# Loads mixed by size, a longer output lag, and one elementwise result kept in PSUM, in a fused attention and feed-forward kernel

## The chip, the cores and the metric

The kernel runs on one core of a Trainium2 chip. The metric is the device time of a run in microseconds (us). Kernels that are compared run on the same chip in the same rounds. A profile also gives the span of one execution; the time is 1.8 to 1.9 us longer than the span.

## The reference, cut to what matters

```python
# q, k, v: (8 batches, 8 heads, 576 positions, 64), float32
mask = np.abs(pos[:, None] - pos[None, :]) <= 32          # a window of 32 to each side
attn = softmax(where(mask, q @ k.T / 8, -1e9)) @ v
x = attn.transpose(0, 2, 1, 3).reshape(4608, 512)
h = x @ w_in                                              # 512 -> 2048
g = where(h >= 1, h, where(h <= -1, 0, (h + 1) ** 2 / 4)) # SMELU
out = g @ w_out                                           # 2048 -> 512, float32
```

The kernel writes SMELU as `min(r, 1) * max(h, r)` with `r = relu(0.5 h + 0.5)`: one ScalarE and two VectorE instructions.

## The kernel before

The main loop has 144 steps (18 blocks of 256 tokens, 8 column blocks of `w_in`). A step makes `hp` (eight matmuls), its SMELU into `gT`, and, LAG steps later, four matmuls into `op`. Attention work for later tokens (`sums`, `scores`) is laid into chosen steps. The mask is added on TensorE up to step 20 (`eng` is None); after that GpSimd multiplies the exponentials by a mask (`eng` is P).

```python
def load_long(b, half, t, eng=None, x=None):      # q or k of one token half: four loads of 72 KB
    ...
    for y in range(NY):
        (eng or nc.gpsimd).dma_start(out=x[32 * y:32 * y + 32], in_=...)
def load_w_in(n, c0=0, c1=512):                   # two loads, each over 64 partitions
    f = slice(512 * n + c0, 512 * n + c1)
    for h in range(2):
        nc.gpsimd.dma_start(out=w_in[64 * h:64 * h + 64, :, f], in_=...)
...
load_v(0, (1,))
load_w_in(0, 0, 256)
load_w_in(0, 256, 512)
load_w_in(1)
load_long(0, 1, 0)
load_long(0, 1, 1)
load_w_in(2)
load_w_in(3)
...
for a in range(NF * NB + LAG):                    # LAG = 12
    t, f = divmod(a, NF)
    eng = None if a < 21 else P
    ...
    if t < NB:
        ...
        hp = ps_h.tile([128, 2, TB], FP, name="hp", tag="hp")       # two buffers in PSUM
        ...                                                         # eight matmuls
        rr = ewp.tile([128, 2, TB], FP, name="rr")
        A.activation(rr, hp, AF.Relu, scale=0.5, bias=0.5)
        mx = ewp.tile([128, 2, TB], FP, name="mx")
        V.tensor_max(mx, hp, rr)
        V.scalar_tensor_tensor(gT[t][:, 2 * f:2 * f + 2], rr, 1.0, mx, op0=ALU.min, op1=ALU.mult)
    ...                                                             # sums and scores of the step
    if a >= LAG:
        for x in range(4 * (a - LAG), 4 * (a - LAG) + 4):
            tt, ff = divmod(x, 2 * NF)
            ...
            nc.tensor.matmul(op, gT[...], w_out[:, ff], start=ff == 0, stop=ff == 2 * NF - 1)
            if ff == 2 * NF - 1:                                    # every fourth step
                osb = osp.tile([128, DM], FP, name="osb")
                A.copy(osb, op)                                     # ScalarE
                nc.sync.dma_start(out=out[128 * tt:128 * tt + 128, :], in_=osb)
```

The softmax here doesn't subtract the row's maximum and nothing guards it: scores larger than these inputs give would overflow.

## Time and profile before

The median is 326.04 us. In the table, "start of step n" is the start of its first `hp` matmul in TensorE's timeline.

| Stage of the kernel before | us from the span's start |
|---|---|
| start of step 0, step 4, step 12 | 19.41, 27.90, 45.36 |
| steps 12 and 13 | 4.67 together |
| steps 14 to 29 | 36.30 |
| step 30 to the start of step 143 | 222.45 |
| start of step 143 to the end | 16.25 |

The prediction shows the page's slices, the waits and the timeline. Two lines of the page's costliest groups matter in addition. In such a line come source line, engine, operation, names and shapes, the count, after the bar the busy us and the mean ns of one, and after the second bar the idle time before them.

```profile
L424 DVE SCALAR_TENSOR_TENSOR gT<-rr,mx 128x512 bf16<-128x512 f32 x144 | 112.9, 784 | 4.9
L423 DVE TENSOR_TENSOR mx<-hp,rr 128x512 f32<-128x512 f32 x144 | 99.1, 688 | 35.5 <-ACT rr L421 34.6
```

The product is slower on average than the max (784 against 688 ns), because some products stand still beside a GpSimd mask.

### The profile page before, as it was taken

How to read it: one execution, taken by the hardware profiler on the slowest of the kernel's cores; microseconds unless marked ns; L12 is line 12 of the kernel's file. 1: busy time of each engine (PE TensorE's matmuls, PEld its weight loads, DVE VectorE, ACT ScalarE, POOL GpSimd, SP SyncE). 2: the span in 40 equal slices, each digit the busy share in tenths (PEclk: the TensorE clock that was granted, in tenths of full speed). 3: DMA queues.
4: the chain of work that ended last, by engine and by line, in shares of the span. 5: the costliest groups of instructions: out<-in, count | busy, mean ns of one | idle time of the engine just before them, and what ended most of it. 6: DMA issues, size and time to landing. Idle time of an engine off the chain costs nothing.

```text
span 325.0 us, 8421 instructions
## 1 busy us (share of the span) xinstructions
PE 301.7 (93%) x3575; PEld 203.2 (63%) x3619; DVE 238.8 (73%) x348; ACT 194.0 (60%) x318; POOL 142.1 (44%) x139
## 2 busy tenths in 40 slices
PE   8596799999999999999999999998999999999995
PEld 3354566666666666666666666666666666666652
DVE  2154787776878798978887787878787877887730
ACT  3455785676765766567655666665676666644421
POOL 8864914666454772457422952178232222100000
PEclk9987999999999999999999999999999999999999
DMA  9999997999969997699750999249960001110011
GB/s 145 117 146 168 127 206 132 147 133 167 84 124 140 88 148 146 89 85 158 127 107 34 120 159 163 58 55 169 138 136 34 34 34 41 52 41 32 34 65 65
DMA packets 129029, 34.52 MB, mean 106 GB/s; under 512 B 117728, under 2 KB 124128, under 8 KB 128992
## 3 DMA queue, kind: packets, MB, share of 16 engines
q0 software_dynamic: 100128, 18.06, 74.5%
q1 hardware_dynamic: 28864, 15.93, 20.4%
q8 instruction: 28, 0.46, 0.6%
q14 instruction: 9, 0.07, 0.1%
HBM read 36.70 MB, written 9.44 MB: 142 GB/s over the span
## 4 chain that ended last, share of the span: by engine, by line
PE 73%; POOL 7%; issue 6%; DVE 5%; DMA 4%; ACT 3%; POOLq 0%; ACTq 0%
PE hp L417 32%; PE op L439 31%; PE bb L280 5%; DMA w_in<-in_moe_w_in_dram 4%; DVE gT L424 2%; POOL vn L105 2%; PE bb L220 2%; DVE mx L423 2%; ACT pt L228 1%; POOL w_in L111 1%; POOL pt L230 1%; POOL kn L87 1%; PE tp L185 1%; POOL qn L95 1%; POOL kn L95 1%
## 5 line engine op out<-in xcount | busy, mean ns | idle before, releaser
L417 PE MATMUL hp<-xT,w_in 128*128 128x256 bf16 x1152 | 150.0, 274 | 5.1 <-DMA w_in<-in_moe_w_in_dram 2.8
L439 PE MATMUL op<-w_out,gT 128*128 128x512 bf16 x534 | 137.5, 379 | 5.8 <-issue 5.4
L417 PEld LDWEIGHTS <-w_in 128*128 128x128 bf16 x1152 | 112.0, 98 | 46.8 <-issue 5.9
L421 ACT ACTIVATE rr<-hp 128x512 f32<-128x512 f32 x144 | 85.8, 596 | 92.1 <-PE hp L417 87.8
L423 DVE TENSOR_TENSOR mx<-hp,rr 128x512 f32<-128x512 f32 x144 | 99.1, 688 | 35.5 <-ACT rr L421 34.6
L424 DVE SCALAR_TENSOR_TENSOR gT<-rr,mx 128x512 bf16<-128x512 f32 x144 | 112.9, 784 | 4.9
L230 POOL TENSOR_TENSOR pt<-pt,mask 128x1024 bf16<-128x1024 bf16 x24 | 53.2, 2218 | 83.9 <-ACT pt L228 79.0
L439 PEld LDWEIGHTS <-gT 128*128 128x128 bf16 x576 | 53.2, 98 | 42.1
L292 DVE TENSOR_TENSOR xT<-bb,rc 128x512 bf16<-128x512 f32 (+1 forms) x32 | 20.9, 653 | 22.7 <-ACT rc L287 22.7
L228 ACT ACTIVATE pt<-bb 128x1024 bf16<-128x1024 f32 (+1 forms) x33 | 33.1, 1011 | 6.8 <-PE bb L220 5.3
L443 ACT COPY osb<-op 128x512 f32<-128x512 f32 x36 | 21.0, 584 | 14.9 <-PE op L439 14.5
L105 POOL DMA_DIRECT2D vn<-in_v_dram x32 | 27.5, 897 | 0.0
L286 ACT ACTIVATE lr<-bb 128x512 f32<-128x512 f32 (+2 forms) x40 | 22.0, 549 | 3.8 <-PE bb L280 3.7
L287 ACT ACTIVATE rc<-lr 128x512 f32<-128x512 f32 (+2 forms) x40 | 23.5, 587 | 1.3
L280 PE MATMUL bb<-pt,ones 64*64 64x256 bf16 (+3 forms) x352 | 20.2, 260 | 2.7 <-POOL pt L230 1.2
L280 PE MATMUL bb<-pt,vn 64*64 64x128 bf16 (+3 forms) x712 | 19.0, 207 | 3.1 <-DMA vn<-in_v_dram 3.1
L248 POOL TENSOR_TENSOR pt<-pt,mask 128x384 bf16<-128x384 bf16 x7 | 6.4, 912 | 30.9 <-ACT pt L246 25.1
L280 PEld LDWEIGHTS <-vn 64*64 64x64 bf16 x712 | 17.3, 110 | 3.3 <-DMA vn<-in_v_dram 3.3
L280 PEld LDWEIGHTS <-ones 64*64 64x64 bf16 x352 | 10.8, 107 | 11.7 <-issue 8.3
L87 POOL DMA_DIRECT2D kn<-in_k_dram x16 | 8.7, 547 | 18.7 <-DMA w_in<-in_moe_w_in_dram 6.7
L95 POOL DMA_DIRECT2D qn<-in_q_dram x12 | 15.0, 1255 | 0.0
L95 POOL DMA_DIRECT2D kn<-in_k_dram x12 | 14.8, 1245 | 0.0
(46 smaller groups left out, 107.2 us busy)
## 6 DMA issues: line engine op xcount, KB each, us to landing
out_dram<-osb SPq DMA_DIRECT2D x36, 256.0 KB, 2.3
vn<-in_v_dram POOLq DMA_DIRECT2D x32, 144.0 KB, 8.1
qn<-in_q_dram POOLq DMA_DIRECT2D x12, 288.0 KB, 6.3
kn<-in_k_dram POOLq DMA_DIRECT2D x12, 288.0 KB, 8.4
w_out<-in_moe_w_out_dram POOLq DMA_DIRECT2D x4, 512.0 KB, 11.0
w_in<-in_moe_w_in_dram POOLq DMA_DIRECT2D x6, 256.0 KB, 7.6
kn<-in_k_dram POOLq DMA_DIRECT2D x16, 72.0 KB, 4.1
qn<-in_q_dram POOLq DMA_DIRECT2D x12, 72.0 KB, 8.0
```

The costliest lines, as they stand in the source:

```text
L95: nc.gpsimd.dma_start(out=x[:, :, h], in_=src[b, NY * h:NY * h + NY].rearrange("y s d -> (y s) d") .rearrange("(u p) d -> p u d", p=128))
L105: nc.gpsimd.dma_start(out=x[64 * a:64 * a + 64, :, h], in_=v[b, y:y + 2].rearrange("y s d -> (y s) d") .rearrange("(c r) d -> r c d", r=64))
L228: A.activation(p, ps[:, :, :128 * n].rearrange(like, y=m), AF.Exp, scale=D ** -0.5)
L230: eng.tensor_mul(p, p, mask4[:, :256 * n].rearrange("p (h j) -> p h j", h=2).rearrange(like, y=m))
L280: nc.tensor.matmul(bb[HD[h], a, o + c0:o + c1], ones[HD[a]] if c is None else vn[b][HD[a], c, h], p(a, h), start=n == 0, stop=True, skip_g ...
L286: A.activation(lr[:, :, :D0], bb[:, :, D0:2 * D0], AF.Ln)
L287: A.activation(rc[:, :, :D0], lr[:, :, :D0], AF.Exp, scale=-1.0)
L417: nc.tensor.matmul(hp[:, j], w_in[:, kk, 256 * f + 128 * j:256 * f + 128 * j + 128], xT[:, kk, r0:r0 + TB], start=n == 0, stop=n == 3)
L421: A.activation(rr, hp, AF.Relu, scale=0.5, bias=0.5)
L423: V.tensor_max(mx, hp, rr)
L424: V.scalar_tensor_tensor(gT[t][:, 2 * f:2 * f + 2], rr, 1.0, mx, op0=ALU.min, op1=ALU.mult)
L439: nc.tensor.matmul(op, gT[tt // 2][:, ff, 128 * (tt % 2):128 * (tt % 2) + 128], w_out[:, ff], start=ff == 0, stop=ff == 2 * NF - 1)
```

## The change

The intent has five parts. (1) All four first `v` loads come earlier, and small loads (72 KB) alternate with large ones in one queue order. (2) The output lag grows from 12 to 14. (3) Batch 2 is also loaded by token halves and transposed on TensorE. (4) The mask stays on TensorE up to step 27. (5) In the step after a GpSimd mask the max overwrites `hp` in PSUM, so that the product has only one input in SBUF.

```diff
-    load_v(0, (1,))
-    load_w_in(0, 0, 256)
-    load_w_in(0, 256, 512)
-    load_w_in(1)
-    load_long(0, 1, 0)
-    load_long(0, 1, 1)
-    load_w_in(2)
-    load_w_in(3)
...
+    for c in range(0, 512, 256):
+        for h in range(2):
+            load_w_in(c, c + 256, h)
+    def mix(small, large):
+        for n in range(0, max(len(small), 2 * len(large)), 2):
+            for fn, *x in large[n // 2:n // 2 + 1] + small[n:n + 2]:
+                fn(*x)
...
+    mix(halves(0, 1), [(load_w_in, c, c + 512, h) for c in (512, 1024, 1536) for h in range(2)])
+    mix(halves(1, 0), [(load_v, 1, n) for n in range(4)])
+    load_w_out(0)
+    load_w_out(1)
+    mix(halves(1, 1), [(load_w_out, 2), (load_w_out, 3)])
+    mix(halves(2, 0), [(load_v, 2, n) for n in range(4)])
...
-    LAG = 12
+    LAG = 14
+    PEM = 28
...
-    for n, a in enumerate((20, 22, 26, 28)):
+    for n, a in enumerate((20, 22, 25, 27)):
         at(a, seq[2 + n][0])
...
-    for n in range(3):
-        tps[23 + n] = [(2, n, t) for t in range(2)]
+    for b, half, *a in ((0, 1, 1, 3), (1, 0, 8, 9), (1, 1, 17, 18), (2, 0, 23, 24), (2, 1, 28, 29)):
+        for t in range(2):
+            tps[a[t]] = [(b, 2 * half + part, t) for part in range(2)]
...
+    masked = [a for a in ev if a >= PEM and any(x[0] is not sums for x in ev[a])]
...
-        eng = None if a < 21 else P
+        eng = None if a < PEM else P
...
-            mx = ewp.tile([128, 2, TB], FP, name="mx")
+            mx = hp if a - 1 in masked else ewp.tile([128, 2, TB], FP, name="mx")
```

More of the change, by code (lines that the diff above doesn't have):

```diff
@@ L45 @@
     PAD = 32
-    LONG, NAT = 2, 3
+    LONG = 3
     const = ctx.enter_context(tc.tile_pool(name="const", bufs=1))
@@ L78, with load_long @@
     qn, kn, vn = {}, {}, {}
-    def load_long(b, half, t, eng=None, x=None):
+    def load_long(b, half, t, y, eng=None, x=None):
         src, dst, nm = ((q, qn, "qn"), (k, kn, "kn"))[t]
-        if x is None:
-            x = nat.tile([128, 2, S], BF, name=nm, tag=nm + "l", bufs=3)
-        dst[b, half] = x
-        for y in range(NY):
-            (eng or nc.gpsimd).dma_start(out=x[32 * y:32 * y + 32],
-                                         in_=src[b].rearrange("(h y) s d -> y h (s d)", h=2)[y]
-                                         .rearrange("h (l p j) -> l p h j", l=2, p=32)[half])
+        if (b, half) not in dst:
+            dst[b, half] = nat.tile([128, 2, S], BF, name=nm, tag=nm + "l", bufs=3) if x is None else x
+        (eng or nc.gpsimd).dma_start(out=dst[b, half][32 * y:32 * y + 32],
+                                     in_=src[b].rearrange("(h y) s d -> y h (s d)", h=2)[y]
+                                     .rearrange("h (l p j) -> l p h j", l=2, p=32)[half])
     def load_nat(b, t):
@@ L96, in load_nat, with load_v, load_w_in @@
                                 .rearrange("(u p) d -> p u d", p=128))
-    def load_v(b, hs=(0, 1)):
+    def load_v(b, n):
         if b not in vn:
             vn[b] = nat.tile([128, 2 * NC, 2, D], BF, name="vn", tag="vn", bufs=3)
-        x = vn[b]
-        for h in hs:
-            for a in range(2):
-                y = NY * h + 2 * a
-                nc.gpsimd.dma_start(out=x[64 * a:64 * a + 64, :, h], in_=v[b, y:y + 2].rearrange("y s d -> (y s) d")
-                                    .rearrange("(c r) d -> r c d", r=64))
-    def load_w_in(n, c0=0, c1=512):
-        f = slice(512 * n + c0, 512 * n + c1)
-        for h in range(2):
-            nc.gpsimd.dma_start(out=w_in[64 * h:64 * h + 64, :, f],
-                                in_=moe_w_in.rearrange("(h y d) f -> h d y f", h=2, d=64)[h][:, :, f])
+        h, a = divmod(n, 2)
+        y = NY * h + 2 * a
+        nc.gpsimd.dma_start(out=vn[b][64 * a:64 * a + 64, :, h], in_=v[b, y:y + 2].rearrange("y s d -> (y s) d")
+                            .rearrange("(c r) d -> r c d", r=64))
+    def load_w_in(c0, c1, h):
+        nc.gpsimd.dma_start(out=w_in[64 * h:64 * h + 64, :, c0:c1],
+                            in_=moe_w_in.rearrange("(h y d) f -> h d y f", h=2, d=64)[h][:, :, c0:c1])
     def load_w_out(n):
@@ L119 @@
     q32 = early.tile([128, 2, S], FP, name="q32")
-    load_long(0, 0, 0, nc.sync, q32)
-    load_long(0, 0, 1)
+    for y in range(NY):
+        load_long(0, 0, 0, y, nc.sync, q32)
+    for y in range(NY):
+        load_long(0, 0, 1, y)
     A.preload_act_table_set("natural_log_exp_and_others")
@@ L125 @@
     V.memset(bias, 0.0)
-    load_v(0, (0,))
     make_identity(nc, ident)
+    for n in range(4):
+        load_v(0, n)
     for h in range(2):
@@ L137, with halves @@
         V.memset(t[:, 0:PAD], 0.0)
-    load_v(0, (1,))
-    load_w_in(0, 0, 256)
-    load_w_in(0, 256, 512)
-    load_w_in(1)
-    load_long(0, 1, 0)
-    load_long(0, 1, 1)
-    load_w_in(2)
-    load_w_in(3)
-    load_long(1, 0, 0)
-    load_long(1, 0, 1)
-    load_v(1)
-    for n in range(4):
-        load_w_out(n)
-    load_long(1, 1, 0)
-    load_long(1, 1, 1)
+    for c in range(0, 512, 256):
[5 more added lines that the diff above has]
+                fn(*x)
+    def halves(b, half):
+        return [(load_long, b, half, t, y) for t in range(2) for y in range(NY)]
+    mix(halves(0, 1), [(load_w_in, c, c + 512, h) for c in (512, 1024, 1536) for h in range(2)])
[4 more added lines that the diff above has]
+    mix(halves(2, 0), [(load_v, 2, n) for n in range(4)])
+    for fn, *x in halves(2, 1):
+        fn(*x)
     kT = {}
@@ L166, in tpose @@
     def tpose(b, n, t, copy, ps):
-        o = qkT(b, t)
-        if b < LONG:
-            half, part = divmod(n, 2)
-            j0, j1 = ((0, 5), (5, 9))[part]
-            src = (qn, kn)[t][b, half]
-            dst = o.rearrange("d (y l p j) -> d l y p j", l=2, p=32, j=9)[:, half, :, :, j0:j1]
-            i = ps[:, :j1 - j0].rearrange("d j (y p) -> d y p j", y=NY)
-        else:
-            j0, j1 = 6 * n, 6 * n + 6
-            src = (qn, kn)[t][b].rearrange("p j h d -> p j (h d)")
-            dst = o[:, 128 * j0:128 * j1]
-            i = ps[:, :6].rearrange("d j p -> d (j p)")
+        half, part = divmod(n, 2)
+        j0, j1 = ((0, 5), (5, 9))[part]
+        src = (qn, kn)[t][b, half]
+        dst = qkT(b, t).rearrange("d (y l p j) -> d l y p j", l=2, p=32, j=9)[:, half, :, :, j0:j1]
         for j in range(j0, j1):
-            if len(src.shape) == 3 and b < LONG and src.shape[1] == 2:
+            if src.shape[1] == 2:
                 for h in range(2):
@@ L187, in tpose @@
                 nc.tensor.transpose(ps[:, j - j0], src[:, j], ident)
-        return lambda: copy(dst, i)
+        return lambda: copy(dst, ps[:, :j1 - j0].rearrange("d j (y p) -> d y p j", y=NY))
     def xpose(b, t):
@@ L386 @@
         at(a, seq[6 + n][0], seq[7 + n][1] if n < len(sl) - 1 else None)
-    for a, b, half, t in ((1, 0, 1, 0), (3, 0, 1, 1), (8, 1, 0, 0), (9, 1, 0, 1), (17, 1, 1, 0), (18, 1, 1, 1)):
-        tps[a] = [(b, 2 * half + part, t) for part in range(2)]
-    for n in range(3):
-        tps[23 + n] = [(2, n, t) for t in range(2)]
+    for b, half, *a in ((0, 1, 1, 3), (1, 0, 8, 9), (1, 1, 17, 18), (2, 0, 23, 24), (2, 1, 28, 29)):
+        for t in range(2):
+            tps[a[t]] = [(b, 2 * half + part, t) for part in range(2)]
     loads, xps = {}, {}
-    for b in range(2, B):
-        a = 12 if b == 2 else sl[5 * (b - 1) - 7] - 17
+    for b in range(LONG, B):
+        a = sl[5 * (b - 1) - 7] - 17
         for t in range(3):
@@ L396 @@
         for t in range(2):
-            if b >= NAT:
-                xps.setdefault(a + 9 + 2 * t, []).append((b, t))
+            xps.setdefault(a + 9 + 2 * t, []).append((b, t))
+    masked = [a for a in ev if a >= PEM and any(x[0] is not sums for x in ev[a])]
     gT = {}
@@ L402 @@
         t, f = divmod(a, NF)
-        eng = None if a < 21 else P
+        eng = None if a < PEM else P
         for b, x in loads.get(a, []):
-            load_nat(b, x) if x < 2 else load_v(b)
+            if x < 2:
+                load_nat(b, x)
+            else:
+                for n in range(4):
+                    load_v(b, n)
         flush()
```

## The prediction

> **What bounds the kernel now.** I read the page first (busy shares and the 40 slices), then TensorE's and GpSimd's waits, then the timeline in four stretches. A "step" below is one turn of the main loop: eight matmuls into `hp` (L417), and from step 12 on four matmuls into `op` (L439) for the step 12 earlier. There are 144 steps, and attention work is put into some of them.
>
> ```profile
> PE 301.7 (93%) x3575; PEld 203.2 (63%) x3619; DVE 238.8 (73%) x348; ACT 194.0 (60%) x318; POOL 142.1 (44%) x139
> ...
> PE   8596799999999999999999999998999999999995
> ...
> PEclk9987999999999999999999999999999999999999
> ...
> GB/s 145 117 146 168 127 206 132 147 133 167 84 124 140 88 148 146 89 85 158 127 107 34 120 159 163 58 55 169 138 136 34 34 34 41 52 41 32 34 65 65
> ```
>
> A slice is 8.1 us. TensorE is full from the seventh slice to the last but one; it has holes, and a clock below full, in the first five. There the transfers move 141 GB/s on average, against 206 in the sixth slice, where the four large `w_out` loads stream. The merged chain shows the steady pace: 0.87 us for `hp` x8 and 0.86 for `op` x4, end to end, so 1.74 us a step, and 2.5 to 2.6 where a step has sums and scores. That stretch is TensorE's own work; only stalls can be won there. The holes have names in the waits, TensorE's over the run, GpSimd's over the first 60 us:
>
> ```profile
> PE bb L280 <- DMA vn<-in_v_dram: 3.1, 1, 3.1
> PE hp L417 <- DMA w_in<-in_moe_w_in_dram: 2.8, 1, 2.8
> ...
> PE hp L417 <- DVE mx L423: 1.1, 2, 0.6
> ```
> ```profile
> POOL kn L87 <- DMA w_in<-in_moe_w_in_dram: 6.7, 7, 1.7
> POOL kn L87 <- DMA w_out<-in_moe_w_out_dram: 4.6, 2, 3.2
> ```
>
> The second fence is GpSimd's queue standing still before it issues a small load: the compiled order has each load wait for the eighth load before it, so only eight are in flight. Eight 72 KB pieces are 0.6 MB, or 2.9 us at 206 GB/s, less than the 4 to 8 us that a load takes from issue to landing; after a run of small loads the engines run dry. From the timeline, the step starts that I build on (4, 8, 12) and one pair of later stalls:
>
> ```profile
> 27.90 1.03 PE L417 MATMUL hp<-xT,w_in 128*128 128x256 bf16 x8 [2.83 <-DMA w_in<-in_moe_w_in_dram]
> ...
> 38.55 1.03 PE L417 MATMUL hp<-xT,w_in 128*128 128x256 bf16 x8 [1.07 <-DVE xT L295]
> ...
> 45.36 1.05 PE L417 MATMUL hp<-xT,w_in 128*128 128x256 bf16 x8
> ```
> ```profile
> 115.46 2.19 POOL L230 TENSOR_TENSOR pt<-pt,mask 128x1024 bf16<-128x1024 bf16 x1
> 115.62 2.59 DVE L424 SCALAR_TENSOR_TENSOR gT<-rr,mx 128x512 bf16<-128x512 f32 x1
> ...
> 120.18 2.13 DVE L424 SCALAR_TENSOR_TENSOR gT<-rr,mx 128x512 bf16<-128x512 f32 x1
> ...
> 123.50 1.03 PE L417 MATMUL hp<-xT,w_in 128*128 128x256 bf16 x8 [0.57 <-DVE mx L423]
> ```
> ```profile
> 309.66 11.39 PE L439 MATMUL op<-w_out,gT 128*128 128x512 bf16 x51
> ```
>
> The VectorE product that takes 0.69 us elsewhere lasts 2.59 and 2.13 us, both times until a GpSimd mask product has ended, and TensorE then waits for VectorE. The last line is the tail, output matmuls alone.
>
> **What the Trainium skill says.** (1) "SBUF — State Buffer", section "Who interferes with whom": a VectorE instruction with two SBUF inputs contends with a GpSimd instruction that reads SBUF, and the later one blocks fully. The trace agrees (2.59 against 0.69 us). With `mx` in PSUM the product has one SBUF input left, so by the same section it is free. (2) "DMA: Bandwidth & Descriptors", section "Anatomy of one DMA — SWDGE (gpsimd) path": some 2 us of each load is fixed and is mostly completion. The trace shows a median of 4.1 us for 72 KB `kn` loads, of which the bytes are 0.36 at 206 GB/s, so depth in flight decides. (3) "TensorE: Matmul & The Clock Gate", Part 1: an idle array falls to half clock. The trace has a granted clock of 0.83 in 10 to 20 us and 0.88 in 30 to 40, and `hp` x8 of step 5 took 1.89 us.
>
> **The change part by part.**
>
> *Queue order.* All four `v` loads now come straight behind the first `k`, ahead of the bias selects, so the last two issue some 1.5 us sooner (8.27 to 6.8) and land, I estimate, at 11.3 us in place of 14.5. The mask then comes 0.8 us later, and its three exponentials end at about 12.6. The first step goes from 19.41 to about 16.5. What sets step 4 is the queue: up to the last `k` of the second half come 512 KB of first `w_in`, four 256 KB pieces and eight 72 KB pieces, 2112 KB or 2.16 MB. With three large and five small in flight (1.1 MB, over 5 us) the queue should not run dry; at 185 GB/s, between 141 and 206, that is 11.7 us, so 23.0. With the transposes (0.69) step 4 starts near 23.6 instead of 27.90: **-4.3 us**. From step 4 to 8 a chain of scores, exponential, sums and xT takes 10.65 us and from 8 to 12 TensorE takes 6.8; neither depends on a load, and the shorter idle time ahead should spare part of the cold clock: **-0.5**. Step 12 starts near 40.6. `w_out` is then landed (about 43 for its last piece, needed three steps after the first).
>
> *Lag of 14.* Steps 12 and 13 (2.34 and 2.33 us) lose 0.86 us of output matmuls each. VectorE needs 0.69 + 0.69 + 0.62 = 2.0 us there and ScalarE 1.7, and two `hp` buffers let TensorE run ahead a little, so I take -0.7 each. The eight matmuls return in the tail at 0.216 each, +1.7. Net **+0.3**.
>
> *Batch 2 by halves.* 72 transposes of half width (18 in 0.69 us) for 36 of full width (12 in 0.68): 2.76 against 2.04, **+0.7** on TensorE, all in full steps. The copies go from 4.0 to 5.9 us on ScalarE and VectorE together, beside TensorE. The loads have rows of 576 elements in place of 64, well ahead of need: nothing on the path.
>
> *Mask on TensorE up to step 27.* Three sets of four more matmuls (steps 21, 26, 27), 0.2 to 0.4 us each: +0.9; three GpSimd products (2.12, 2.44 and 0.91) and the waits behind them go, -0.3. Net **+0.6**.
>
> *Max in PSUM.* The stalls at steps 45 and 47 (0.25 and 0.73 over the usual) and the same pair at 62 and 64 follow from two blocked products each and go: -2.0. The 0.9 at step 99 comes of loads ahead of the mask on GpSimd and stays. But `hp` is now held to the end of the product instead of the max. In steps after a mask that end is 3.2 to 3.8 us after the step's start, and the buffer is wanted again 3.48 us after it: I count some eight such steps with 0.05 to 0.3 us each, +0.6. Net **-1.4**.
>
> Sum: -4.3 - 0.5 + 0.3 + 0.7 + 0.6 - 1.4 = **-4.6 us**, 326.0 to **321.4 us**.
>
> **The rivals.** *A, the start is bandwidth, not depth.* The share of the DMA engines is 9 in most early slices, and if this means real transfer, the order only permutes landings: the second-half `k` now lies behind `w_in`, and step 4 gains only what `v` gains, 1.5 to 2 us. Against it: 141 against 206 GB/s, and GpSimd's idle time. It makes about 324. *B, the whole front moves.* The chain of 10.65 us is mostly latency and cold clock; warm, with `w_in` early, it could lose 1 to 2 us more, and if steps 12 and 13 lose their full 0.86, the lag is free: 318.5 to 319.5. For it: `hp` x8 at 1.89 us is twice the warm 0.87. *C, PSUM gives back what it takes.* If holding `hp` longer stalls TensorE after each of some 29 masks by 0.1 us, or the max is slower into PSUM, the -1.4 becomes +1 and the total about 324. Against it: most products end 0.2 us or more ahead of need.
>
> **Range and chances.** The front carries most: -2 to -7. The rest sums to +0.2 with an uncertainty of 1.5. I take 318.0 to 324.7 for 8 in 10. Faster by over 2% means below 319.5, which needs most of B: 0.24. Slower than 332.6 would need a transfer landing after its use (the halves of batch 2 wait for buffers freed at steps 1 to 9): 0.02. Within 2%: 0.74.
>
> **What would show it.** Right: the wait for `vn` gone or under 1 us; step 4 near 23.6 and step 12 near 40.6; over 160 GB/s in slices 2 to 5; no product over 1.5 us at steps 43, 45, 60 and 62; steps 12 and 13 at 1.5 to 1.8 us; a tail of 59 output matmuls, 13.1 us; new waits of `hp` for the product under 1 us in total. Wrong: step 4 still at 26 or later (A); step 12 at 39 or earlier (B); waits of `hp` on VectorE of 2 us or more (C); or a stop at steps 17 to 29 for a transpose whose load has not landed, which no part of the sum has.

## The result and the profile after

The changed kernel took **328.01 us** (327.99 to 328.12, 4 runs), the kernel before 326.19 us in the same rounds (325.83 to 326.64, 4 runs). The ratio is 1.0056, with a 95% interval of 1.0038 to 1.0073. Here and below, a ratio is the mean time of one kernel's fast runs over that of the other's of the same rounds, so it is not quite the ratio of the medians quoted. The change costs half a per cent; the prediction had 321.4 us and a range that ended at 324.7.

From the page of the changed kernel: first the busy shares and slices, then the groups of the max and of the product.

```profile
PE 305.1 (94%) x3625; PEld 202.9 (62%) x3667; DVE 233.8 (72%) x350; ACT 194.1 (60%) x319; POOL 139.7 (43%) x148
...
PE   8959799999999999999999999998999999999995
...
PEclk9978999999999999999999999999999999999999
...
GB/s 144 133 170 161 143 205 161 143 170 103 107 69 143 87 142 119 126 96 139 67 145 42 150 176 128 34 89 162 155 90 36 34 34 33 34 32 60 38 66 64
```
```profile
L423 DVE SCALAR_TENSOR_TENSOR gT<-rr,mx 128x512 bf16<-128x512 f32 x116 | 86.5, 746 | 4.0
...
L423 DVE SCALAR_TENSOR_TENSOR gT<-rr,hp 128x512 bf16<-128x512 f32 x28 | 19.3, 688 | 1.0
L422 DVE TENSOR_TENSOR hp<-hp,rr 128x512 f32<-128x512 f32 x28 | 19.4, 692 | 2.4 <-ACT rr L419 2.4
```

TensorE has become 3.4 us busier (301.7 to 305.1): that is added work. VectorE is 5 us less busy (238.8 to 233.8), as intended: the 28 products that read `hp` take 688 ns each. But VectorE is not what the end of the kernel waits for. The rate in slices 2 to 5 (133, 170, 161, 143) is 152 GB/s on average, against 140 in the kernel before (117, 146, 168, 127); the prediction wanted over 160.

TensorE's waits in the changed kernel, in us in total, times, and longest:

```profile
PE tp L179 <- DMA qn<-in_q_dram: 3.4, 1, 3.4
PE bb L274 <- POOL pt L224: 1.2, 3, 0.9
...
PE hp L415 <- DVE gT L423: 1.2, 6, 0.3
```

The old waits for `vn` (3.1) and `w_in` (2.8) are gone or nearly so. In their place stands one wait of 3.4 us for `qn`, and a wait of `hp` for the product, which did not exist before. The stages, from the two timelines:

| | before | after | difference |
|---|---|---|---|
| start of step 0 | 19.41 | 15.31 | -4.10 |
| start of step 4 | 27.90 | 26.76 | -1.14 |
| start of step 12 | 45.36 | 43.23 | -2.13 |
| steps 12 and 13 | 4.67 | 2.93 | -1.74 |
| steps 14 to 29 | 36.30 | 37.84 | +1.54 |
| step 30 to the start of step 143 | 222.45 | 224.17 | +1.72 |
| start of step 143 to the end | 16.25 | 17.99 | +1.74 |

These sum to +1.13. Of the remaining 0.7 us between the medians, 0.6 are no part of the change: the profiled run of the kernel before took 326.80 us, above its median of 326.19. A second trace of the old load order (before_mask28, below) has 17.64, 27.38 and 45.12 in the first three rows, so the gain at step 0 is less certain than that at step 12.

The timeline of TensorE in the changed kernel's front (start, duration, operation, and in brackets the idle time before it with its releaser) shows what became of the 4.1 us won at step 0:

```profile
21.00 1.17 PE L179 MATMUL tp<-ident,qn 128*64 128x128 bf16 x18 [3.39 <-DMA qn<-in_q_dram]
...
25.86 0.97 PE L179 MATMUL tp<-ident,kn 128*64 128x128 bf16 x18 [0.16 <-DMA kn<-in_k_dram]
26.76 1.05 PE L415 MATMUL hp<-xT,w_in 128*128 128x256 bf16 x8
```

TensorE begins earlier and then stands 3.39 us for the second half of `q`. The last `k` landed at 25.72, and step 4 follows it. The tail has exactly the 59 output matmuls expected:

```profile
309.05 13.11 PE L438 MATMUL op<-w_out,gT 128*128 128x512 bf16 x59
```

### The profile page after: what moved, and what is told of

Read it like the earlier page. It is cut to its first block, busy times and chain, and to the rows that moved or that the text cites. A ratio compares the mean times of both kernels' runs of the same rounds, so it can differ in the third digit from the quotient of the medians.

```text
span 326.2 us, 8539 instructions
## 1 busy us (share of the span) xinstructions
PE 305.1 (94%) x3625; PEld 202.9 (62%) x3667; DVE 233.8 (72%) x350; ACT 194.1 (60%) x319; POOL 139.7 (43%) x148
## 4 chain that ended last, share of the span: by engine, by line
PE 59%; POOL 15%; issue 9%; ACT 8%; DVE 4%; DMA 4%; ACTq 0%; POOLq 0%
PE hp L415 26%; PE op L438 25%; PE bb L274 5%; POOL pt L224 4%; POOL vn L101 4%; ACT pt L222 3%; POOL kn L93 2%; DMA w_in<-in_moe_w_in_dram 2%; PE bb L214 2%; ACT rr L419 2%; DVE gT L423 2%; DMA kn<-in_k_dram 2%; POOL qn L93 2%; PE tp L179 1%; DVE hp L422 1%
## 5 line engine op out<-in xcount | busy, mean ns | idle before, releaser
L422 DVE TENSOR_TENSOR mx<-hp,rr 128x512 f32<-128x512 f32 x116 | 80.1, 690 | 38.0 <-ACT rr L419 37.0
L423 DVE SCALAR_TENSOR_TENSOR gT<-rr,mx 128x512 bf16<-128x512 f32 x116 | 86.5, 746 | 4.0
L224 POOL TENSOR_TENSOR pt<-pt,mask 128x1024 bf16<-128x1024 bf16 x22 | 48.2, 2190 | 93.9 <-ACT pt L222 93.9
L422 DVE TENSOR_TENSOR hp<-hp,rr 128x512 f32<-128x512 f32 x28 | 19.4, 692 | 2.4 <-ACT rr L419 2.4
L423 DVE SCALAR_TENSOR_TENSOR gT<-rr,hp 128x512 bf16<-128x512 f32 x28 | 19.3, 688 | 1.0
L85 POOL DMA_DIRECT2D kn<-in_k_dram x24 | 13.1, 552 | 11.9 <-DMA w_out<-in_moe_w_out_dram 3.9
L242 POOL TENSOR_TENSOR pt<-pt,mask 128x384 bf16<-128x384 bf16 x6 | 5.5, 912 | 26.4 <-ACT pt L240 26.4
```

The lines of the kernel that those rows point to most:

```text
L224: eng.tensor_mul(p, p, mask4[:, :256 * n].rearrange("p (h j) -> p h j", h=2).rearrange(like, y=m))
```

## The experiments

Fifteen kernels ran. "This" is the median of the kernel named, "before" that of the kernel before in the same rounds. All gave a correct result but the one marked.

### What costs 1.7 us in the steady part?

In the changed kernel some steps take 2.02 to 2.17 us where 1.74 is usual: 47 (which took 2.47 before), 51, 67, 75, 115 among them. They lie two steps after steps such as 45, 49, 65, 73 and 113, in which GpSimd masks and which are 1 modulo 4. With a lag of 14 the output copies of ScalarE fall on steps that are 1 modulo 4; with 12 they fell on 3 modulo 4. The timelines of step 50, the step after a mask, in the kernel before:

```profile
127.87 1.04 PE L417 MATMUL hp<-xT,w_in 128*128 128x256 bf16 x8
...
129.20 0.58 ACT L421 ACTIVATE rr<-hp 128x512 f32<-128x512 f32 x1
...
131.34 0.38 PE L417 MATMUL hp<-xT,w_in 128*128 128x256 bf16 x2
```

and in the changed kernel:

```profile
125.60 1.04 PE L415 MATMUL hp<-xT,w_in 128*128 128x256 bf16 x8
...
126.93 0.57 ACT L442 COPY osb<-op 128x512 f32<-128x512 f32 x1
...
127.39 0.60 ACT L419 ACTIVATE rr<-hp 128x512 f32<-128x512 f32 x1
...
128.76 0.69 DVE L423 SCALAR_TENSOR_TENSOR gT<-rr,hp 128x512 bf16<-128x512 f32 x1
...
129.51 1.05 PE L415 MATMUL hp<-xT,w_in 128*128 128x256 bf16 x8 [0.27 <-DVE gT L423]
```

Before, the Relu starts 1.33 us after its step and step 52 comes 3.47 us after step 50. After, the copy is ahead of the Relu, which starts at 1.79; the product that now holds `hp` ends at 129.45, 3.85 us after the step's start, and step 52, which wants that buffer, comes 3.91 us after step 50. My theory from this was that the max in PSUM and the place of the copies together make the loss. Three runs undo one part each: the lag, the max, the copy.

**lag12**

```diff
-    LAG = 14
+    LAG = 12
```

> The changed kernel with an output lag of 12 again, all else kept. Theory 1: the loss of 1.7 us from step 30 to step 143 comes of two parts together: hp is held to the end of the product in the step after a mask, and a lag of 14 puts ScalarE's output copies on steps 1 mod 4, which are many of the masked ones (45, 49, 65, 73, 77, 81, 113). Then with a lag of 12 the long steps 51, 67, 75, 79, 83 and 115 (2.02 to 2.17 us) go back to 1.74, new ones of 2.0 to 2.2 come two after masked steps that are 3 mod 4 (41, 61, 101, 105), and steps 30 to 143 take about 223.0 us instead of 224.2. Steps 12 and 13 take 2.33 again (+1.7), the tail is 1.74 shorter. Total 326.8 against 328.0. Rival (the max in PSUM costs by itself, whatever the lag): the same steps stay long, 328.0.

Measured: 326.62 us (before 325.77), ratio 1.0031, interval 1.0003 to 1.0059. Steps 12 and 13 went back to 4.67 us and the tail to 16.25: the lag itself gives 1.74 us and takes 1.74. From step 30 to 143 the span fell from 224.17 to 222.65, so there, with the max in PSUM, the lag of 14 costs 1.52 us. Steps 47, 51, 67 and 75 were normal again, and 41, 61, 101 and 105 became long (1.95 to 2.16), two after masks at 39, 59, 99 and 103, all 3 modulo 4. The long steps follow the copies.

**max_sbuf**

```diff
-            mx = hp if a - 1 in masked else ewp.tile([128, 2, TB], FP, name="mx")
+            mx = ewp.tile([128, 2, TB], FP, name="mx")
```

> The changed kernel with the max always in SBUF. Theory 1: steps 51, 67, 75, 79, 83 and 115 go back to 1.74 (-2.0 us), and the blocked products at 43 and 60 come back with long steps 47 and 64 (+0.4 and +0.7): steps 30 to 143 take 223.0 to 223.3, total about 327.0. Rival (the max in PSUM is worth what it removes and the loss is elsewhere): total 328.5 or more.

Measured: 327.13 us (before 325.77), ratio 1.0041, interval 1.0018 to 1.0063. Steps 51, 67, 75, 79 and 115 went back to 1.74, step 83 stayed long (2.47), and the stalls at 47 and 64 returned (2.47 each). From step 30 to 143: 223.55, so with the copies where they are the max in PSUM costs 0.6 us net where it was to gain 1.4.

**osb_late**

```diff
             A.activation(rr, hp, AF.Relu, scale=0.5, bias=0.5)
+            put_out()                  # the copy and store held back from the step before
...
-                    A.copy(osb, op)
-                    nc.sync.dma_start(...)
+                    held.append((tt, op))
...
```

> The changed kernel with each output copy of ScalarE put behind the ReLU of the next step, so that it no longer delays that ReLU; lag 14 and the max in PSUM stay. Theory 1: the products after masks end at 3.2 to 3.5 us after the step's start everywhere, steps 47, 51, 67, 75, 79, 83 and 115 take 1.74 to 1.80, steps 30 to 143 take 222.0 us, total about 325.8. Rival (PSUM itself): long steps stay, 328.

Measured: 325.55 us (before 325.77), ratio 0.9992, interval 0.9964 to 1.0021. From step 30 to 143: 221.91, 2.26 less than in the changed kernel, and the long steps are gone. The same step 50 in its timeline:

```profile
127.20 0.58 ACT L428 ACTIVATE rr<-hp 128x512 f32<-128x512 f32 x1
...
127.67 0.58 ACT L401 COPY osb<-op 128x512 f32<-128x512 f32 x1
...
129.40 1.05 PE L424 MATMUL hp<-xT,w_in 128*128 128x256 bf16 x8
```

The step starts at 125.87, so the Relu is at 1.33 again, and step 52 follows at 3.53.

**osb_sbuf** completes the square: the copies late and the max in SBUF (both edits above).

> Output copies behind the next ReLU, and the max always in SBUF. It completes the square: with the copies where the change puts them, the max in PSUM cost 0.6 us from step 30 to 143 (224.2 against 223.6). Theory 1 (PSUM removes the blocked products, worth 1.5 us or more, and costs only where ScalarE is late): here steps 30 to 143 take 223.0 to 223.6 us against 221.9 with the max in PSUM. Rival (the max in PSUM is worth nothing in itself): 222.0, the same.

Measured: 326.71 us (before 326.27), ratio 1.0011, interval 0.9972 to 1.0049. From step 30 to the start of step 143, in us:

| | copy ahead of the Relu | copy behind the Relu |
|---|---|---|
| max in SBUF | 223.55 | 222.84 |
| max in PSUM | 224.17 | 221.91 |

With the copies out of the way the max in PSUM gains 0.93 us; with the copies ahead it loses 0.62. These differences are far above the scatter: this stretch takes 224.10 to 224.15 us in seven other runs with the same loop from step 30 on, and 221.87 and 221.91 in two more with the late copies. The stall that PSUM takes away comes back here, at step 48 (TensorE's timeline of osb_sbuf):

```profile
121.70 1.03 PE L424 MATMUL hp<-xT,w_in 128*128 128x256 bf16 x8 [0.57 <-DVE mx L432]
```

Even so 0.93 is less than the 2.0 that I had counted. The pair at steps 45 and 62 did not move (2.80 each before, 2.81 and 2.80 after; 2.58 and 2.57 with the lag of 12, where GpSimd runs 0.2 us earlier against the step). GpSimd's timeline in the changed kernel shows why:

```profile
110.20 3.42 POOL L101 DMA_DIRECT2D vn<-in_v_dram  x4
113.58 2.19 POOL L224 TENSOR_TENSOR pt<-pt,mask 128x1024 bf16<-128x1024 bf16 x1
```

The mask product stands behind four loads that GpSimd issues, ends at 115.77, and the sums of step 45 start at 115.83. No VectorE product is in that chain. A part of the stage lies elsewhere: step 30 takes 2.93 us in place of 2.55 in osb_late, osb_sbuf and max_sbuf as in the changed kernel. Without this 0.38, osb_sbuf is at 222.46, the 222.45 of the kernel before. No run was made for it, but TensorE's timeline of the changed kernel names the wait:

```profile
85.34 0.29 PE L274 MATMUL bb<-pt,ones 64*64 64x224 bf16 x4 [0.29 <-DVE kT L182]
```

The sums of step 30 wait for VectorE's copy of the new transposes of step 29. So this part belongs to the halves of batch 2, not to the max.

### What holds the front?

The bytes between the last `v` (11.16) and the last `k` of the second half (25.72) are 2112 KB in 14.56 us, or 148 GB/s; the prediction had 185. (The first of these bytes move before the last `v` lands, so this is no pure rate: in v_late, with `v` landing at 13.61, the stretch is 12.04 us, and `k` lands at 25.65 all the same.) Six runs have these loads in this order (the changed kernel, lag12, max_sbuf, osb_late, osb_sbuf, pem21): step 4 starts at 25.88 to 26.95, 26.48 in the mean, and step 12 at 43.16 in the mean. That is the scatter against which the next runs are to be read.

**unmixed** issues the same loads in runs, large ones and then small ones, up to batch 2, the four `v` still early.

```diff
-    mix(halves(0, 1), [(load_w_in, c, c + 512, h) for c in (512, 1024, 1536) for h in range(2)])
+    run([(load_w_in, 512, 1024, h) for h in range(2)])
+    run(halves(0, 1))
+    run([(load_w_in, c, c + 512, h) for c in (1024, 1536) for h in range(2)])
...
```

> The changed kernel with the loads in runs again (two w_in, eight small, four w_in, eight small, v, four w_out, the small of batches 1 and 2), all else kept. Theory 1 (the start is set by how fast the bytes move, about 150 GB/s, not by how many loads are in flight): step 4 starts within 0.7 us of the 26.8 of the changed kernel, total within 0.7 us of it. Rival, my prediction (depth in flight): the queue runs dry again before the third w_in pair, step 4 starts at 28.5 or later and the total is about 2 us longer, 330.

Measured: 327.88 us (before 325.77), ratio 1.0067, interval 1.0042 to 1.0093, the time of the changed kernel. Step 4 starts at 27.60, between the two expectations. Mixing did change the front. From 16 to 24 us the loads move at 138 GB/s here, and at 144 and 147 in the two traces of the old order, but at 165 to 185 in the six mixed runs; the last load that step 4 needs lands at 27.47 here and at 25.02 to 26.19 there. Step 4 keeps about 1.1 us of that, because in the mixed order the transposes of `k` still follow, and the total shows nothing. Whether the depth of the queue or the mixture itself raised the rate is not shown.

**v_late** issues two of the first `v` loads ahead of the identity and two behind the bias selects.

```diff
     make_identity(nc, ident)
-    for n in range(4):
-        load_v(0, n)
...
+    for n in range(2, 4):
+        load_v(0, n)               # behind the bias selects
```

> The changed kernel with the four v loads of batch 0 where they were before, two ahead of the identity and two behind the bias selects. My theory (these loads are what moved the first step from 19.4 to 15.3 us, and the order of the others did nothing): the first step starts at 18.5 to 19.5 us, step 4 at 27.5 to 28.5, total 1 to 2 us longer than the changed kernel, 329 to 330. Rival (the start is a fixed number of bytes, the order within it does not matter): step 4 within 0.5 us of 26.8, total within 0.7 us.

Measured: 327.82 us (before 326.40), ratio 1.006, interval 0.9995 to 1.0125. Step 0 starts 1.6 us later (16.93), and step 4 at 26.41 all the same. My expectation that the early `v` carries the front's gain fell. What comes first does not matter while step 4 waits for all of the bytes.

**w_in_wide** loads the first 512 columns in two loads with rows of 512 elements, in place of four with rows of 256. The bytes are the same.

```diff
-    for c in range(0, 512, 256):
-        for h in range(2):
-            load_w_in(c, c + 256, h)
+    for h in range(2):
+        load_w_in(0, 512, h)
```

> The changed kernel with the first 512 columns of w_in loaded in two pieces of 256 KB (rows of 512 elements) instead of four of 128 KB (rows of 256). Theory (rows of 256 elements move slower: in the changed kernel 512 KB took from 11.2 to 16.4 us): they land 1 to 2 us earlier, the first q of the second half near 19.5 instead of 20.9, step 4 near 25.5, total 1 us shorter. Rival (the 3.2 us hole in the landings at 12 to 15 us is not of the rows): within 0.5 us of the changed kernel.

Measured: 326.40 us (before 326.40), ratio 1.0000, interval 0.9956 to 1.0044. Step 4 starts at 25.03:

```profile
24.41 0.69 PE L178 MATMUL tp<-ident,kn 128*64 128x128 bf16 x18 [1.98 <-DMA kn<-in_k_dram]
25.03 1.05 PE L414 MATMUL hp<-xT,w_in 128*128 128x256 bf16 x8
```

It is the only one of these three edits that brings step 4 forward beyond the scatter. The trace's packet records suggest a reason. A row of a tile is one packet; its median time is 32 ns for 128 bytes, 60 for 512, 98 for 1024 and 107 for 1152, the same in the kernels before and after. That is about 22 ns a row plus 0.074 ns a byte. The 2112 KB are 1024 rows of 512 bytes, 1024 of 1024 and 512 of 1152, together 217 us of packets, or 13.5 us on each of 16 engines: my estimate from those records, against 14.56 measured. It is rough, for it lays the packets of an engine end to end, and the trace has them overlap (a DMA share of 1.20 from 9 to 27 us). Wide rows take 0.7 us off it; the stretch took 13.46 us in this run (10.81 to 24.27) and 14.05 in osb_wide below, against 13.86 to 15.15 in the six. That there are two loads in place of four is a rival which no run separates from the rows.

**w_in_128** asks whether the number of partitions counts as well. The Trainium skill, "SBUF — State Buffer", section "Door 1: The DMA port swizzle", says that a transfer's rate depends on how many of 16 ports its partitions reach, and 64 partitions in a row reach half of them. Every `w_in` load here covers 128 partitions with rows as before, **with a wrong result** (rows land on other partitions; relative error 0.030).

```diff
-        nc.gpsimd.dma_start(out=w_in[64 * h:64 * h + 64, :, c0:c1],
-                            in_=moe_w_in.rearrange("(h y d) f -> h d y f", h=2, d=64)[h][:, :, c0:c1])
+        nc.gpsimd.dma_start(out=w_in[:, 2 * h:2 * h + 2, c0:c1],
+                            in_=moe_w_in.rearrange("(y p) f -> p y f", p=128)[:, 2 * h:2 * h + 2, c0:c1])
```

> Gives a wrong result on purpose (rows of w_in fall on other partitions; no work changes). Every load of w_in keeps its bytes, its number of pieces and its row of 256 or 512 elements, but covers 128 partitions and two of the four groups of rows in place of 64 partitions and all four. Theory P (the number of partitions that a load covers sets its rate: loads over 32 or 64 partitions run at about 150 GB/s in the front, those of w_out over 128 at about 205): step 4 comes 1.5 us or more sooner than 26.76, near 25.0, and the 2112 KB before it take 13 us or less in place of 14.56; about 326.3 us. Rival R (row length): the rows are as before, step 4 within 0.5 of 26.76, about 328.0 us.

Measured: 328.41 us (before 325.83), ratio 1.0083, interval 1.0054 to 1.0112. Step 4 starts at 27.22, and packets take 60 and 98 ns as before. Theory P falls: the number of partitions that a load covers is not what limits these loads.

**w_in_y** was to change both: four loads for the first 512 columns, each over 128 partitions with rows of 512 elements, and a correct result.

```diff
-    for c in range(0, 512, 256):
-        for h in range(2):
-            load_w_in(c, c + 256, h)
+    for y in range(4):
+        nc.gpsimd.dma_start(out=w_in[:, y, 0:512],
+                            in_=moe_w_in.rearrange("(h y d) f -> y h d f", h=2, d=64)[y][:, :, 0:512])
```

> Correct result. Only the first 512 columns of w_in, 512 KB, still in four loads: each is one group of rows over 128 partitions with rows of 512 elements, in place of 64 partitions with four rows of 256. Theory P and rival R both expect a gain here; against w_in_wide (step 4 at 25.03, two loads of 64 partitions, 326.4 us) P expects step 4 another 0.5 us sooner or more, R the same 25.0.

Measured: 332.02 us (before 325.83), ratio 1.0196, interval 1.0154 to 1.0237. It fits neither theory: step 4 starts at 30.68, and TensorE's waits have a new line.

```profile
PE hp L415 <- DMA w_in<-in_moe_w_in_dram: 5.8, 2, 4.0
```

The experiment failed as a test, because more than rows and partitions changed. The four loads landed at 16.98 to 21.72 in place of 12.06 to 16.43, and the trace has 3584 more packets of 4 bytes, seven for each of the 512 rows. Otherwise there are 16 such packets a load (192 more after the change than before it, with 12 more loads), so it looks as if this source pattern, with the partitions split in two groups, had been cut into small transfers; that is inferred, not shown. From 11 to 13 us the DMA engines have a share of 0.57 and move 28 GB/s (1.23 and 152 in the changed kernel), so a poor spread over the engines is a rival, and no run tells the two apart.

**osb_w_in_y** has the same loads together with the late copies.

> w_in_y together with osb_late, to see whether it beats osb_wide (324.7 us, ratio 0.9956). Under P about 324.2 us, under R 324.7; steps from 30 to 143 again 221.9 us.

Measured: 330.46 us (before 325.83), ratio 1.014, interval 1.0097 to 1.0182. The loads are as bad here, and the steps from 30 to 143 take 221.87 us again, a second sign that the late copies do what osb_late showed.

**front** puts the small loads ahead of the large `w_in` pieces, and the transposes, scores and sums that stood at steps 1 to 6 at steps 1 to 3.

```diff
-    mix(halves(0, 1), [(load_w_in, ...) ...])
+    for fn, *x in halves(0, 1) + [(load_w_in, c, c + 512, h) for c in (512, 1024, 1536) for h in range(2)]:
+        fn(*x)
...
-    at(4, (scores, 0, (0, 1), (0, 2), (2, 4)), (scores8, 0, ps_n))
+    at(1, (scores, 0, (0, 1), (0, 2), (2, 4)), (scores8, 0, ps_n))
...
```

> The changed kernel with the eight small loads of the second half of batch 0 ahead of the large w_in loads, and with the transposes and scores of that half at step 1 (sums at 2 and 3), instead of steps 1 to 6. Theory (the chain from the second half's k over scores, exponential, sums and xT to step 8 is about 10 us, and it starts late because k lands at 25.7): k lands near 20, the chain runs beside the w_in loads, steps 2 to 7 follow the landings of w_in (last near 31), step 8 starts near 33 to 34 instead of 36.4, total 2.5 to 3 us shorter, 325.0 to 325.5. Rival (w_in's landings are the bound and only come later): step 8 at 36 or later, total as the changed kernel or longer.

Measured: 326.34 us (before 326.40), ratio 1.0006, interval 0.9959 to 1.0052. Step 8 starts at 34.04, 2.4 us sooner than in the changed kernel. But a later stop takes part of it back: step 17 lasts 3.77 us in place of 2.46, for the last of `w_out`, which landed at 51.50.

```profile
51.54 1.02 PE L453 MATMUL op<-w_out,gT 128*128 128x512 bf16 x4 [1.16 <-DMA w_out<-in_moe_w_out_dram]
```

A front that asks for the same bytes sooner meets the same transfers later.

### The masks, and the fastest version

**pem21** takes back only the masks on TensorE: `PEM = 21` in the changed kernel.

> The changed kernel with the masks of steps 21, 26 and 27 on GpSimd again (and, by the kernel's own rule, the max of steps 22, 27 and 28 in PSUM). My sum had +0.6 us for moving them to TensorE. If right: steps 14 to 30 take 37.2 us instead of 37.8, total 0.6 shorter. Rival (the GpSimd masks are late because 24 loads of batches 2 and 3 stand ahead of them in the same queue): a sum waits for its mask at steps 27 to 30 by 1 us or more, total 328.5 or more.

Measured: 329.85 us (before 326.40), ratio 1.0107, interval 1.0061 to 1.0152. Step 27 takes 4.55 us in place of 2.77, since the sum waits for a GpSimd mask:

```profile
PE bb L274 <- POOL pt L224: 3.2, 4, 1.9
```

**before_mask28** does the part alone in the kernel before: `eng = None if a < 28 else P`.

> The kernel before with one edit: masks on TensorE up to step 27 instead of step 20. My sum had +0.6 us for it (0.9 of matmuls, less 0.3 of waits). In the changed kernel the opposite edit lost 1.5 us by a wait for a GpSimd mask. If that wait is of the new load order alone, this one is 0.3 to 0.9 slower than the kernel before (steps 14 to 30 take 36.6 to 37.2 instead of 36.3); if the mask move is a gain in itself, it is 0.5 or more faster.

Measured: 327.02 us (before 326.27), ratio 1.0028, interval 0.9981 to 1.0075. Steps 14 to 29 take 36.82 in place of 36.30: the masks cost 0.52 us of TensorE there, near the +0.6 predicted. In the changed kernel they are needed nevertheless, with its sums and transposes moved; which of those moves makes the mask late there was not tried. This run also shows what the granted clock (the share of TensorE's full clock that the profile shows) does to the front. In both traces of the old order TensorE has half its clock for 3.4 us after step 4: in the kernel before in steps 4 to 8 (granted clock 0.84, 10.65 us), here in steps 8 to 12 (0.80, 8.22 us in place of 6.81). In five of the six traces of the new order it falls, as good as all of it, before step 4, where TensorE waits for loads anyway, and steps 4 to 8 take 9.59 to 9.88; in osb_late it falls later (10.80). So about 1 us of the 2.1 gained by step 12 is of the clock, and two traces of the old order are too few to say whether the load order decides it.

**osb_wide** joins the two edits that helped, the late copies and the wide rows.

> The changed kernel with two of the edits that helped alone: output copies behind the next ReLU, and the first 512 columns of w_in in two loads with rows of 512 elements. If the two gains are of separate stretches (step 30 to 143: -2.3 us; start to step 4: -1.7 us) they add up: 324.0 us against 328.0 of the changed kernel and 326.2 of the kernel before, so faster than both. If the start only varies from run to run: 325.6.

Measured: **324.74 us** (before 326.27), ratio 0.9956, interval 0.991 to 1.0002. It is the fastest median, about 1% below the changed kernel; against the kernel before, the interval just includes no difference. Its step 4 starts at 25.70, also ahead of all six runs with narrow rows.

**front_lag16** adds the order of front, a lag of 16, and `q` and `k` of batch 1 ahead of `w_out`.

> Everything that helped in one kernel: output copies behind the next ReLU, wide first w_in, the second half of batch 0 ahead of the large w_in loads with its transposes and scores at step 1, the small loads of the second half of batch 1 ahead of w_out, and an output lag of 16 so that w_out is needed two steps later. If the loads of the first 50 us are the bound up to step 17, moving w_out's first use and the small loads takes away the 1.3 us stop that the reordered kernel had at step 17: step 8 near 33, step 17 without a stop, total 321.5 to 323. If the bytes are simply late by then: a stop of 1 to 3 us moves to steps 16 to 19 and the total is 324 to 325.

Measured: 325.23 us (before 326.27), ratio 0.9968, interval 0.9934 to 1.0003. Step 12 starts at 40.90, and step 17 no longer stops. But step 16 waits 0.80 us for VectorE's `xT`, not for a load, steps 30 to 143 take 222.80 in place of 221.91, and the tail is 19.69, again 1.70 us longer for two more steps of lag. It does not beat osb_wide.

## Why the prediction was wrong

- **Queue order (-4.3) and warm clock (-0.5): measured -2.1 in all**, by the start of step 12. The step that failed is "at 185 GB/s, between 141 and 206, that is 11.7 us, so 23.0": the term was mis-sized. The stretch took 14.56 us at 148 GB/s. Mixed loads did reach 165 to 185 GB/s from 16 to 24 us; from 8 to 16 us, where the 512-byte rows of the first `w_in` move, the six runs had 130 to 137. The reason given, depth in flight, stays open: mixing brought the last needed load some 2 us forward, of which step 4 kept 1.1 (unmixed). Rival A was nearer with its 1.5 to 2 us at step 4 (1.1 measured) but not right in its cause, for it gave all of the gain to `v`, and v_late has step 4 as early with `v` late. The clock term was right in kind; about 1 us of the -2.1 fits it, and may be chance. The last piece of `w_out` landed at 50.07, not near 43; TensorE shows no wait for it.
- **The first `v`: right, and worth little.** It landed at 11.16 as estimated, and step 0 came at 15.31, earlier than the 16.5 predicted. Then TensorE waited for `qn`. Removing the first wait of a chain whose later wait ends at a fixed time gives only what that later wait leaves (v_late).
- **Lag of 14 (+0.3): its two terms cancel, measured 0.0.** Steps 12 and 13 lost 0.87 us each, not 0.7 (rival B had that), and the tail grew by 1.74. What the sum did not have is that the lag also chooses the steps in which ScalarE copies, which cost 1.52 us from step 30 to 143 (lag12).
- **Halves of batch 2 (+0.7) and masks to step 27 (+0.6): together +1.54** in steps 14 to 29, 1.3 predicted. The masks alone were 0.52 in the kernel before, and the rest was not measured by itself. The 0.38 of step 30 comes on top: "the copies ... beside TensorE" failed there, where the sums wait for such a copy.
- **Max in PSUM (-1.4): the sign failed.** Steps 30 to 143 took +1.72, of which 0.38 lies in step 30 and belongs to the transposes. The rest is a miss as large as that of the front: +1.34 in place of -1.4. Of the stalls, those at 47 and 64 went (-0.41 and -0.73), those at 45 and 62 did not: "follow from two blocked products each and go" was wrong for them, for there the sum waits for the mask itself. The other term, "some eight such steps with 0.05 to 0.3 us each", had the mechanism and not the size: 0.3 to 0.43 us a step, because the copies' new place delays the Relu by 0.46 us in just those steps. Rival C expected this stall, and gave +1; but the max into PSUM is not slower (692 against 688 ns).

The parts failed together. Putting the copies behind the Relu wins 2.26 us with the max in PSUM (224.17 to 221.91) and 0.71 with it in SBUF (223.55 to 222.84); the other 1.55 us arise only where the copies that the longer lag has moved meet a PSUM buffer held 0.7 us longer. What remains open: the exact cost of the new transposes, why mixing raised the rate and what sets it from 8 to 16 us, and why single packets in the front last 0.3 to 2 us (53 between 8 and 26 us after the change, 32 before), which the sum by row does not contain.

## What to carry to other kernels

Before holding a buffer longer, write down for each step when it is released and when it is next wanted, with everything that the releasing engines have queued in that step; here 0.5 us of ScalarE work, moved by a change of the lag, decided the sign. Before borrowing a rate from other loads, hold it against the rate of the same stretch in the trace and against its packets by row length, and find the last wait of the chain before counting what the first one is worth. When a step's start waits for a sum, ask what the sum waited for before blaming the engine that was slow beside it.

## What the Trainium skill lacked or had wrong

- "DMA: Bandwidth & Descriptors", section "Why small descriptors are slow (HBM only)", names a fixed overhead of about 3 cycles a packet, which it puts at 27% for 256 bytes. In these float32 to bfloat16 loads the packets took 32, 60, 98 and 107 ns for 128, 512, 1024 and 1152 bytes, so about 22 ns do not depend on the bytes: more than a third of a 512-byte row. The page has no time by row length for such loads.
- The same page, section "Anatomy of one DMA — SWDGE (gpsimd) path": from its fixed part of a load I concluded that depth in flight decides. The page does not say so, and the total did not show it: mixed and unmixed orders gave 328.0 and 327.9 us.
- "SBUF — State Buffer", section "Door 1: The DMA port swizzle": by its count of ports a load over 128 partitions should beat one over 64. Here it did not (step 4 at 27.22 against 26.76, at about 148 GB/s), so the ports were not the limit of these loads.
- The same page, section "Who interferes with whom", was right: products with one input in SBUF took 688 ns each beside GpSimd, where products with two had taken up to 2.59 us.
- "Perfetto Trace Analysis", section "Optimizing Scalar/DVE Operations", gives VectorE a larger overhead on PSUM than on SBUF (about 125 against 60 ns). For a max that reads `hp` in PSUM in both cases, writing to PSUM in place of SBUF made no difference of that size: 692 against 688 ns.
- No page tells that a source pattern with the partitions in two groups can multiply the packets: 3584 more of 4 bytes for 512 KB (w_in_y).
